# A fused attention, soft mixture of experts and gated output kernel: the last tile's scores moved ahead, seven groups of unread products taken out, another order of the tail, and another pace of weight loads

## The chip, the cores and the metric

The kernel runs on one core of a Trainium2 chip. The metric is the time of one execution on the device, in microseconds (us); of several runs the median counts. A core has five engines that run their own queues of instructions in order and wait for each other by semaphores: TensorE (PE in the profile; PEld is its loading of weights), VectorE (DVE), ScalarE (ACT), GpSimd (POOL) and SyncE (SP), whose queue here holds nothing but the issues of data transfers (DMA).

## What is computed

The reference has three stages: an attention within chunks of 64 positions, a soft mixture of 8 experts with 4 slots each, and a feed-forward layer whose hidden values go through a softmax gate and a normalisation.

```python
# attention: 8 x 8 heads, 576 positions in chunks of 64, head size 64
attn = softmax(q_c @ k_c.T / sqrt(64)); x = attn @ v_c            # -> x: 4608 x 512
# soft mixture of experts, phi: 512 x 32
logits = x @ phi
d = exp(logits - logits.max(0)); d /= d.sum(0) + 1e-09             # over all 4608 tokens
slot_input = d.T @ x                                               # 32 slots x 512
for e in range(8):                                                 # 512 -> 1024 -> 512
    slot_out[e] = relu(slot_input[e] @ w1[e]) @ w2[e]
c = exp(logits - logits.max(1)); c /= c.sum(1) + 1e-09
x = c @ slot_out
# feed-forward with a softmax gate
h = x @ w_in; solu = h * softmax(h)
ln = (solu - mean) / sqrt(var + 1e-06) * g_ln
out = ln @ w_out
```

The softmax over all tokens (`d`) means that no expert can start before every tile of the attention has been seen.

## The kernel before, in words

**The loop (to about 130 us).** The 4608 tokens are 36 tiles of 128 (`NT = 36`). Step i of the loop, for i from 0 to 33, works on several tiles at once: scores S of tile i (`pe_S`, TensorE), row maxima, subtraction and exponential (`mx`, `sub` on VectorE, `exp` on ScalarE), transposed probabilities of tile i-1 (`PT`, evacuated by `PTe`), the product with the values of tile i-2 (`x`, with its row sums `rz`, their reciprocal `rc` and the scaling `xm`), and the transposition and logits of tile i-3 (`xT`, `xTe`, `LT`). Every four tiles a block of logits is closed by a running maximum, an exponential and a product with x that is added up in `acc`. Beside that, GpSimd, ScalarE and VectorE turn the output layer's weights into another format (`sq`, `t`, `u`, `m`, `a`, `add`, `mul`). `STEP` gives the order of these operations for four steps, after which it repeats.

**The loads.** All transfers are issued from SyncE, in the order of the program: q and k of tile i+4 (`qk`, two halves of 256 KB), values for two tiles (`v`, 520 KB), output weights (`raw`, 512 KB), and the experts' weights: 64 tiles `w` of 512 KB. At each step `W` issues `PACE[i+1] - PACE[i]` of these 64. They go into a ring of 23 buffers; the next 19 go into buffers of the loop as these are given up (the operations `own_c`, `own_q`, `own_v`, `own_p`, `own_t`, `own_x`), and the last 22 into ring buffers that the experts have read. A transfer whose buffer is still being read blocks every transfer behind it in SyncE's queue.

**The tail (126 to 148 us), written out by hand.** The steps of the last tiles are single operations with names, registered by `op(name, names of what must stand ahead)`; the string `ORDER` lists them all, and they are emitted in that order. So `ORDER` sets the order of each engine's queue, and nothing else does. The names that matter here:
- S34, S35: scores of the last two tiles. mx34, sub34, exp34; mx35 and, in halves, sub350, sub351, exp350, exp351. PT33, PT34, PT350, PT351 and ptev..: transposed probabilities and their evacuation on ScalarE. x32 to x34, x350, x351: the products with the values. rz.., ev..: row sums (ScalarE), then reciprocal and scaling (VectorE). xT.., xtev.., LT..: transposition, its evacuation, logits.
- lte7, L7, lall7, tm7 close block 7; lte8, L8, lall8, tm8 and lte83, L83, lall83 close block 8; mT8, mn8, Ls, mnl find the maximum, mb spreads it, d7, d8 subtract it, de7, de8 take the exponential, mc and al give the factor for what was summed before. sl70 to sl81 and z8 are the products with d, acc80, acc81 and zacc8 add them up, zt, zr, si0, si1 and siT give the experts' input.
- hz0, hz1 write zeros into two banks of PSUM (ScalarE). px closes a pool and emits nothing.
- id0 to id6: products of the unit matrix with itself, written into places of PSUM that nothing reads before they are written again.
- cq1 to cq7 (GpSimd) sum the output weights, cm0 and cm1 (TensorE) average them, cme (VectorE) copies the average, cms0 to cms7 (GpSimd) subtract it from the 8 blocks of weights, px0 to px7 (VectorE) take each block's largest value, px8 the largest of these, wmt (TensorE) transposes it and wmv (VectorE) makes the scale of it.

**The experts (148 to 187 us).** Two groups of four experts; each `w1_..` or `w2_..` is 8 instructions of 4 x 512, four experts side by side in the array. Between them stand the transpositions of the hidden values, and on VectorE the combine weights (cz0 to cz5) and the maxima px. In `ORDER` this part reads, in the kernel before:

```python
... zr si0 si1 siT open2 cm1 w1_000 w1_001 cme rl00 w1_010
cz0 cms2 cms3 ht00 w1_011 he00 cms6 cz1 cms4 rl01 px2 w2_000 cms7 ht01 px7 w2_001 cms0 cz2 cz3 px6 cz4 cms5 px3 cz5
he01 w2_010 w2_011 so0 px4 px5 cms1 w1_100 px1 w1_101 px0 sot0 late ch0 cl0 px8 wmt ch2 cl2 wmv ct0 ch1 w1_110 rl10
```

**The output layer (to the end).** For each tile: hidden values h, exponential, gate, two 16 bit parts, their transposition by DMA, and 24 products of 128 x 512 (L1396), then the output.

Of the kernel before, what the change touches and what calls it, by code (L numbers as in the profile page):

```python
# [44 lines left out]
ORDER = """
cq1 cq2 cq3 cq4 cq5 cq6 cq7 S34 loadw xT31 PT33 xtev31 x32 own_c mx34 rz32 LT31 sub34 ev32 S35 ptev33 lte7 mx35 exp34
sub350 PT34 x33 ptev34 xT32 L7 exp350 rz33 xtev32 own_q sub351 x34 ev33 PT350 exp351 id0 rz34 ptev0 xT33 PT351 LT32
lall7 tm7 x350 ptev1 x351 xtev33 ev34 xT34 LT33 id1 xtev34 own_v rz35 rc35 LT34 id2 ev350 ev351 xT350 px lte8 xT351
id4 xtev350 xtev351 L8 tm8 LT35 id5 mT8 lte83 mn8 own_p Ls L83 id6 own_t mnl hz1 lall83 mb lall8 cm0 mc id3 d7 d8 de7
hz0 sl71 de8 al sl70 own_x z8 sl80 zacc8 sl81 zt acc80 acc81 zr si0 si1 siT open2 cm1 w1_000 w1_001 cme rl00 w1_010  # L50
cz0 cms2 cms3 ht00 w1_011 he00 cms6 cz1 cms4 rl01 px2 w2_000 cms7 ht01 px7 w2_001 cms0 cz2 cz3 px6 cz4 cms5 px3 cz5
he01 w2_010 w2_011 so0 px4 px5 cms1 w1_100 px1 w1_101 px0 sot0 late ch0 cl0 px8 wmt ch2 cl2 wmv ct0 ch1 w1_110 rl10
cl1 hi0 ct1 ch3 hi1 lo0 ht10 he10 ch4 cl3 ce0 hi6 ce1 ct2 ce2 w1_111 cpt cpe rl11 ch5 wc48 hi3 ct3 ht11 hi4 cl4 ce3
hi5 wc49 hi7 cl5 ct4 lo3 wc50 wc51 ch6 he11 ce4 cl6 wc52 wc53 lo2 ct6 wc54 wc55 ch8 ct5 hi2 ce6 soc0 wc56 soe0 wc57
ch7 soct0 cl7 ct7 ce5 ce7 wc58 cl8 wc59 soce0 wc60 wc61 soc2 soct2 wc62 wc63 soc3 lo1 sw0 soct3 soce2 sw1 soce3 sw2
pev0 pev1 ct8 end2 ce8 f_open f_turn f_h0 f_m0 f_h1 f_m1 f_mm f_e0 f_sc f_g1 f_g0 rp0 f_dg f_e1 f_u0 f_T0 f_u1 s4h0
f_k0 f_T1 f_Te0 f_k1 f_Te1 B0a f_km f_ul0 f_E f_ul1 rp1 s4h1 B0b B0c B0d f_s1 Av1 s4l0 s4l1 Au1 Hm2 B0 Hm3 Al1 Hx2 Hs2
He2 Aq1 B1 f_mean Av2 Au2 f_v1 Hx3 Hm4 He3 Al2 Hs3 Av3 Hx4 Au3 B2 f_v0 S0 Al3 As1 He4 Hm5 Aq2 Av4 C0 Aq3 Hm6 Hs4 Hx5
Hs5 Au4 C1 Al4 As2 He5 Av5 B3 Au5 Hx6 He6 As3 Hm7 Hs6 Aq5 Al5 Aq4 Av6 Au6 B4 C2 As4 Hx7 As5 He7 Hs7 Al6 Av7 Au7 C3 Aq6
Aq7 As6  # L60
"""


# [1437 lines left out]
```

## Time and profile before

| | us |
|---|---|
| median of 3 runs | 404.35 |
| lowest, highest | 404.04, 406.44 |
| the profiled execution, in all | 406.2 |
| its span, first to last instruction | 404.4 |

Busy time in the profiled execution: TensorE 385.9 us (95% of the span), VectorE 311.5 (77%), ScalarE 223.8 (55%), GpSimd 199.4 (49%). The data engines move 407 to 411 GB/s in most slices up to 182 us, and 130 to 166 after it.

Times in the rows count from the span's start. A row of the timeline gives start, duration, engine, line, operation, what is written and read, shapes and the number of instructions merged; the bracket behind it says how long the engine was idle before it and what ended that. Matmuls are pipelined, and their ends are modelled: a row overlaps the next one a little. A float32 matmul of the program is two rows' worth of instructions in the trace.

### The profile page before, as it was taken

To read this page: it belongs to the slowest core of one execution; us is meant where nothing else is said; L and a number is where in the kernel's file an instruction comes from. 1 tells how busy PE (TensorE), PEld (TensorE's weight loads), DVE (VectorE), ACT (ScalarE), POOL (GpSimd) and SP (SyncE) were. 2 spreads that over 40 slices of the span, in tenths; PEclk is the share of its full clock that TensorE was granted. 3 is DMA by queue.
4 is the path that set the end of the run, shared out by engine and by line. 5 is a ranking of instruction groups with operands and counts; after the bars stand their busy time and mean duration, and the time that the engine had idled before them with its cause. 6 is when DMAs were issued, how large, how long until landed. Compare 5 with 4: busy or idle time off the path is not lost. (4 is left out here: it accounts for less than half of the span.)

```text
span 404.4 us, 10343 instructions
## 1 busy us (share of the span) xinstructions
PE 385.9 (95%) x3961; PEld 223.0 (55%) x3961; DVE 311.5 (77%) x777; ACT 223.8 (55%) x470; POOL 199.4 (49%) x201
## 2 busy tenths in 40 slices
PE   3798999999999999999999999999999999999997
PEld 2676777877787752355544444444444444444445
DVE  3588788888987447683989789999888888888840
ACT  1487777877776512231576765556545545455521
POOL 2377677777778428240113235555545445454430
PEclk9999999999999999999999999999999999999999
DMA  7999999999999999993056756778657786567661
GB/s 231 361 411 409 407 407 408 409 397 387 403 361 347 404 398 402 408 410 82 15 98 151 130 134 140 166 166 160 144 132 135 156 130 143 133 143 156 131 157 52
DMA packets 101153, 99.20 MB, mean 245 GB/s; under 512 B 78064, under 2 KB 78704, under 8 KB 101104
## 3 DMA queue, kind: packets, MB, share of 16 engines
q1 hardware_dynamic: 101104, 98.54, 77.9%
q8 instruction: 31, 0.51, 0.5%
q14 instruction: 18, 0.15, 0.1%
HBM read 70.60 MB, written 9.44 MB: 198 GB/s over the span
## 5 line engine op out<-in xcount | busy, mean ns | idle before, releaser
L1197 POOL TENSOR_SCALAR uh<-u,sc 128x1024 f16<-128x1024 f32 (+1 forms) x35 | 65.0, 1857 | 51.2 <-issue 38.3
L1396 PEld LDWEIGHTS <-uhT 128*128 128x128 f16 x560 | 52.2, 98 | 68.6 <-issue 9.0
L1396 PE MATMUL o_ps<-xb,uhT 128*128 128x512 f16 x280 | 66.6, 380 | 0.8 <-DMA uhT<-uh 0.8
L1396 PE MATMUL o_ps<-xb,ulT 128*128 128x512 f16 x280 | 66.3, 379 | 0.0
L1396 PE MATMUL o_ps<-wo,uhT 128*128 128x512 f16 x280 | 66.1, 379 | 0.0
L1325 ACT ACTIVATE e<-h_ps,nm 128x1024 f32<-128x1024 f32 x34 | 37.8, 1112 | 43.9 <-DVE nm L1319 43.9
L1213 ACT ACTIVATE e<-u,nmean 128x1024 f32<-128x1024 f32 x35 | 40.1, 1147 | 28.7 <-DVE nmean L1212 28.7
L257 PE MATMUL s_ps<-qk 128*64 128x128 f32 x576 | 42.4, 291 | 10.8 <-DMA qk<-in_qkT 7.3
L1363 POOL TENSOR_TENSOR a<-a,mhalf 128x1 f32<-128x1 f32 x36 | 21.7, 604 | 56.6 <-DVE a L1380 42.7
L1319 DVE TENSOR_REDUCE nm<-h_ps 128x1 f32<-128x1024 f32 x34 | 41.5, 1220 | 9.7 <-PE h_ps L1314 9.7
L1188 DVE SCALAR_TENSOR_TENSOR u<-h_ps,e 128x1024 f32<-128x1024 f32 x35 | 42.8, 1223 | 6.1 <-ACT e L1325 6.1
L1396 PEld LDWEIGHTS <-ulT 128*128 128x128 f16 x280 | 27.3, 98 | 33.1 <-issue 0.3
L1373 DVE SCALAR_TENSOR_TENSOR ul<-u,sc,uh 128x1024 f16<-128x1024 f32 x35 | 45.3, 1295 | 0.0
L257 PEld LDWEIGHTS s_ps<-qk 128*64 128x64 f32 x576 | 33.1, 144 | 17.9 <-issue 12.1
L266 DVE TENSOR_REDUCE mx<-s_ps 128x8 f32<-128x512 f32 x36 | 24.7, 685 | 12.5 <-PE s_ps L257 12.3
L399 ACT ACTIVATE xt_b<-xt_ps 128x512 f32<-128x512 f32 (+1 forms) x37 | 21.5, 584 | 17.3 <-PE xt_ps L417 16.5
L220 POOL TENSOR_SCALAR conv<-conv 128x256 f32<-128x256 f32 x16 | 17.5, 1096 | 24.6 <-ACT conv L207 24.6
L1414 ACT ACTIVATE ob<-o_ps,a 128x512 f32<-128x512 f32 x35 | 23.7, 678 | 9.5 <-PE o_ps L1396 8.0
L1314 PE MATMUL h_ps<-s,c4T 128*128 128x512 f32 x68 | 27.6, 488 | 0.0
L278 ACT ACTIVATE p<-p 128x512 f32<-128x512 f32 x35 | 21.7, 620 | 6.7 <-DVE p L272 6.7
L272 DVE TENSOR_TENSOR p<-s_ps,mx 128x512 f32<-128x512 f32 x35 | 24.1, 690 | 0.9
L230 POOL TENSOR_TENSOR conv<-conv 128x256 int32<-128x256 int32 x32 | 23.3, 727 | 2.6
(234 smaller groups left out, 637.8 us busy)
## 6 DMA issues: line engine op xcount, KB each, us to landing
w<-in_w SPq DMA_DIRECT2D x45, 512.0 KB, 8.3
qk<-in_qkT SPq DMA_DIRECT2D x72, 256.0 KB, 7.0
vall<-in_v SPq DMA_DIRECT2D x18, 520.0 KB, 7.6
out<-ob SPq DMA_DIRECT2D x35, 256.0 KB, 2.1
raw<-in_w SPq DMA_DIRECT2D x16, 512.0 KB, 7.6
qk<-in_w SPq DMA_DIRECT2D x4, 512.0 KB, 9.6
w_raw<-in_w SPq DMA_DIRECT2D x3, 512.0 KB, 9.3
vall<-in_w SPq DMA_DIRECT2D x3, 512.0 KB, 9.0
```

The lines of the kernel that those rows point to most:

```text
L257: nc.tensor.matmul(s[ts(c, 64), ts(g, 128)], b[:, 1, ts(2 * g + c, 64)], b[:, 0:3:2, ts(2 * g + c, 64)], start=True, stop=True, tile_posit ...
L266: mark("mx", nc.vector.tensor_reduce(out=mx, in_=s, axis=AX.X, op=ALU.max))
L272: mark("sub", nc.vector.tensor_tensor(out=p, in0=s, in1=mx.unsqueeze(2).to_broadcast([128, 8, 64]), op=ALU.subtract,))
L1188: nc.vector.scalar_tensor_tensor(out=u, in0=d["h"], scalar=1.0, in1=e, op0=ALU.mult, op1=ALU.mult, accum_out=zz[:, 1:2])
L1197: nc.gpsimd.tensor_scalar(out=uh[:, 0:n], in0=u[:, 0:n], scalar1=d["sc"][:, 1:2], scalar2=1.0, op0=ALU.mult, op1=ALU.mult)
L1213: nc.scalar.activation(out=d["e"], in_=d["u"], func=AF.Square, bias=nmean, scale=1.0, accum_out=d["zz"][:, 2:3])
L1314: nc.tensor.matmul(h[:, ts(n, 512)], c4T[:, i, :], s4[n], start=True, stop=True)
L1319: nc.vector.tensor_reduce(out=nm, in_=st[i]["h"], axis=AX.X, op=ALU.max, negate=True)
L1325: nc.scalar.activation(out=d["e"], in_=d["h"], func=AF.Exp, bias=d["nm"], scale=1.0, accum_out=d["zz"][:, 0:1])
L1373: nc.vector.scalar_tensor_tensor(out=ul, in0=d["u"], scalar=d["sc"][:, 1:2], in1=d["uh"], op0=ALU.mult, op1=ALU.subtract)
L1396: nc.tensor.matmul(d["o"], lt(n % 8), w(n % 8), start=(n == 0), stop=(n == 23))
L1414: nc.scalar.activation(out=ob, in_=d["o"], func=AF.Copy, scale=d["a"][:, 7:8])
```

## The change

Four edits, all in tables and in the tail; no operation of the computation is added or removed.

1. `ORDER`: S35 stands directly behind S34, and the list from there to the experts' first products is another one. Among what moved: mx35 ahead of sub34; x33 ahead of PT34; rz34 and ev34 ahead of tm7, which now stands behind ev351; xT34 ahead of x351; d7 ahead of mc; al and de8 ahead of hz0; z8 between sl80 and sl81; cm1 behind w1_000 and w1_001, where it stood ahead of both. From cme on the list is the same.
2. The operations id0 to id6 and the function `idle` are gone: 12 products of 128 x 128 on TensorE.
3. `PACE` is raised by one or two tiles at most of its entries from 18 to 33. Entry 34 and the ring of 23 are the same.

```diff
 PACE = [
-    0, 0, 1, 1, 2, 3, 3, 4, 4, 5, 6, 6, 7, 7, 8, 9, 9, 10, 10, 11, 12, 12, 13, 13, 14, 15, 15, 16,
-    16, 17, 18, 18, 19, 22, 25, 25,
+    0, 0, 1, 1, 2, 3, 3, 4, 4, 5, 6, 6, 7, 7, 8, 9, 9, 10, 11, 11, 12, 13, 14, 14, 15, 16, 16, 17,
+    18, 19, 19, 20, 21, 23, 25, 25,
 ]
...
-cq1 cq2 cq3 cq4 cq5 cq6 cq7 S34 loadw xT31 PT33 xtev31 x32 own_c mx34 rz32 LT31 sub34 ev32 S35 ptev33 lte7 mx35 exp34
...
+cq1 cq2 cq3 cq4 cq5 cq6 cq7 S34 S35 loadw xT31 mx34 mx35 PT33 x32 xtev31 rz32 ptev33 sub34 LT31 lte7 ev32 own_c exp34
...
-    def idle(o, n):
-        for _ in range(n):
-            nc.tensor.matmul(o, ident, ident, start=True, stop=True)
-
-    op("id0", "PT350")(lambda: idle(T["pt"][:, 2, :], 2))
-    op("id1", "LT33 id0")(lambda: idle(lt_t[last][:, 3, :], 2))
-    op("id2", "LT34 id1")(lambda: idle(lt_t[last][:, 3, :], 2))
-    op("id4", "xT351 ev34 id2")(lambda: idle(sx[:, 0, 256:384], 1))
-    op("id5", "LT35 id4")(lambda: idle(sx[:, 0, 256:384], 1))
-    op("id6", "L83 lte8 id5")(lambda: idle(lt_t[last][:, 0, :], 2))
-    op("id3", "cm0 mnl ev34 id2")(lambda: idle(sx[:, 0, 256:384], 2))
```

Line numbers of the changed kernel are one smaller up to here and twelve smaller behind the removed lines.

**VectorE in the tail.** The names: mx are the maxima (mx34, mx35), `p<-s_ps,mx` is sub34, `xl` are the halves of tile 35, RECIPROCAL and the row behind it are ev32, ev33 and ev34, `tm<-L_ps` is tm7. In the kernel before:

```order
L266 TENSOR_REDUCE mx<-s_ps 128x8
L272 TENSOR_TENSOR p<-s_ps,mx 128x512
L604 RECIPROCAL rz<-rz 128x8
L607 TENSOR_TENSOR xb_84<-x_ps,rz 128x2x4x64
L266 TENSOR_REDUCE mx<-s_ps 128x8
L545 TENSOR_TENSOR xl_152<-s_ps,mx 128x256
L545 TENSOR_TENSOR xl_153<-s_ps,mx 128x256
L604 RECIPROCAL rz<-rz 128x8
L607 TENSOR_TENSOR xb_85<-x_ps,rz 128x2x4x64
L366 TENSOR_REDUCE tm<-L_ps 128x32
L604 RECIPROCAL rz<-rz 128x8
L607 TENSOR_TENSOR xb_86<-s_ps,rz 128x2x4x64
```

In the changed kernel:

```order
L265 TENSOR_REDUCE mx<-s_ps 128x8 x2
L271 TENSOR_TENSOR p<-s_ps,mx 128x512
L603 RECIPROCAL rz<-rz 128x8
L606 TENSOR_TENSOR xb_84<-x_ps,rz 128x2x4x64
L544 TENSOR_TENSOR xl_153<-s_ps,mx 128x256
L544 TENSOR_TENSOR xl_152<-s_ps,mx 128x256
L603 RECIPROCAL rz<-rz 128x8
L606 TENSOR_TENSOR xb_85<-x_ps,rz 128x2x4x64
L603 RECIPROCAL rz<-rz 128x8
L606 TENSOR_TENSOR xb_86<-s_ps,rz 128x2x4x64
```

Both maxima now stand together, and tm7 no longer stands between ev33 and ev34 (xb_85 and xb_86).

**TensorE at the start of the experts.** `s_ps<-cs,acc` is si0 and si1, `cm_ps` is cm1, `h_ps<-w,xl` are the first products with experts' weights (16 of them are w1_000 and w1_001). In the kernel before:

```order
L846 MATMUL zt_ps<-cs,zacc 128x32
L857 MATMUL s_ps<-cs,acc 128x32 x4
L827 MATMUL cm_ps<-csum,mean_l 128x256
L939 MATMUL h_ps_2581<-w,xl_152 4x512 x16
L939 MATMUL h_ps_2582<-w,xl_152 4x512 x8
L964 MATMUL hT_ps<-cs,xb_85 128x128 x4
```

In the changed kernel:

```order
L834 MATMUL zt_ps<-cs,zacc 128x32
L845 MATMUL s_ps<-cs,acc 128x32 x4
L927 MATMUL h_ps_2567<-w,xl_152 4x512 x16
L815 MATMUL cm_ps<-csum,mean_l 128x256
L927 MATMUL h_ps_2568<-w,xl_152 4x512 x8
L952 MATMUL hT_ps<-cs,xb_85 128x128 x4
```

cm1 moved behind the first 16 products with weights.

**SyncE at the end of the loop.** qk are loads of q and k (the last row of them, qk3, is tile 35), vall of values, w of experts' weights. In the kernel before:

```order
L177 DMA qk0_111<-in_qkT 64x1024 x2
L129 DMA w_1993<-in_w12 128x1024
L182 DMA vall_123<-in_v1 128x1040
L177 DMA qk1_112<-in_qkT 64x1024 x2
L129 DMA w_2051<-in_w12 128x1024
L177 DMA qk2_113<-in_qkT 64x1024 x2
L182 DMA vall_123<-in_v1 128x1040
L177 DMA qk3_114<-in_qkT 64x1024 x2
L129 DMA w_2209<-in_w12 128x1024
```

In the changed kernel:

```order
L176 DMA qk3_114<-in_qkT 64x1024 x2
L128 DMA w_1940<-in_w12 128x1024
L176 DMA qk0_111<-in_qkT 64x1024 x2
L128 DMA w_1997<-in_w12 128x1024
L181 DMA vall_123<-in_v1 128x1040
L176 DMA qk1_112<-in_qkT 64x1024 x2
L176 DMA qk2_113<-in_qkT 64x1024 x2
L128 DMA w_2117<-in_w12 128x1024
L181 DMA vall_123<-in_v1 128x1040
L176 DMA qk3_114<-in_qkT 64x1024 x2
L128 DMA w_2213<-in_w12 128x1024
```

One more w stands ahead of qk0 (tile 32), one behind qk2 (tile 34) where none stood, and of the five that followed qk3 (tile 35) three are left.

## Rows read from the trace of the kernel before

**Rows 1.** The chain that ended last (start us, us, what), its long run of products

```profile
210.10 5.35 PE o_ps L1396 x24
```

**Rows 2.** Busy time by stretches: PE, PEld, DVE, ACT, POOL; PEclk, DMA share, GB/s

```profile
0.00:20.00 20.00, 11.18 (x140) 9.11 (x141) 9.12 (x19) 6.03 (x13) 5.67 (x14) 1.00 0.85 295
...
115.00:120.00 5.00, 4.97 (x105) 4.17 (x105) 4.26 (x10) 3.80 (x12) 3.70 (x5) 1.00 0.92 332
120.00:125.00 5.00, 4.77 (x103) 3.32 (x100) 4.83 (x15) 3.58 (x11) 3.98 (x5) 1.00 0.86 303
...
155.00:160.00 5.00, 5.00 (x48) 1.38 (x44) 4.96 (x6) 2.28 (x3) 5.00 (x4) 1.00 1.03 406
160.00:165.00 5.00, 5.00 (x52) 1.23 (x48) 4.93 (x10) 1.08 (x3) 0.05 (x1) 1.00 1.02 405
```

**Rows 3.** Timeline of TensorE in the tail: S34, and the unread product id2

```profile
126.02 1.09 PE L257 MATMUL s_ps<-qk 128*64 128x128 f32 x16
...
138.17 0.71 PE L646 MATMUL lt_ps<-cs 128*128 128x128 f32 x4
```

**Rows 4.** Timeline of ScalarE in the tail: rz34, lall7, lte8, hz0, al

```profile
133.77 0.19 ACT L305 ACTIVATE rz<-s_ps 128x8 f32<-128x8 f32 x1
...
134.61 0.27 ACT L361 ACTIVATE lall<-L_ps 128x128 f32<-128x128 f32 x1
...
138.98 0.49 ACT L346 ACTIVATE ltb<-lt_ps 128x384 f32<-128x384 f32 x1 [1.39 <-PE lt_ps L646]
...
143.48 0.58 ACT L817 ACTIVATE h_ps<-cs 128x512 f32<-128x512 f32 x1
...
144.20 0.28 ACT L457 ACTIVATE al<-mc 128x1 f32<-128x1 f32 x1
```

**Rows 5.** Timeline of VectorE in the tail: tm7, then the reciprocal of ev34

```profile
134.92 0.29 DVE L366 TENSOR_REDUCE tm<-L_ps 128x32 f32<-128x128 f32 x1 [0.78 <-ACT lall L361]
135.12 0.19 DVE L604 RECIPROCAL rz<-rz 128x8 f32<-128x8 f32 x1
```

**Rows 6.** Timeline from cm1 to wmt: TensorE, VectorE and GpSimd

```profile
147.49 0.68 PE L827 MATMUL cm_ps<-csum,mean_l 128*128 128x256 f32 x2
148.10 5.33 PE L939 MATMUL h_ps<-w,xl 128*4 128x512 f32 x48
...
147.69 0.29 DVE L863 TENSOR_TENSOR xl<-s_ps,zr 128x128 f32<-128x128 f32 x1 [0.25 <-PE s_ps L857]
148.21 0.69 DVE L400 COPY acc<-cm_ps 128x512 f32<-128x512 f32 x1 [0.22 <-PE cm_ps L827]
...
148.98 11.07 POOL L834 TENSOR_TENSOR wo<-wo,acc 128x512 f32<-128x512 f32 x8 [13.19 <-DVE acc L400]
...
156.35 1.27 DVE L1059 TENSOR_REDUCE wmx<-wo 128x1 f32<-128x512 f32 x2
...
165.26 0.15 DVE L1066 TENSOR_REDUCE wmx<-wmx 128x1 f32<-128x8 f32 x1
...
167.17 0.14 PEld L1071 LDWEIGHTS wm_ps<-cs,wmx 128*128 128x128 f32 x1
```

**Rows 7.** Loads of tile 29 and of the last weights, and who reads them

```profile
L177 SPq DMA_DIRECT2D qk<-in_qkT x2: 477/480/484, 98.1 to 98.8; - x2
DMA to landing us min/median/max: 7.6/7.6/7.6
...
107.76 1.09 PE L257 MATMUL s_ps<-qk 128*64 128x128 f32 x16
...
L129 SPq DMA_DIRECT2D w<-in_w x1: 327/327/327, 174.9 to 174.9; - x1
DMA to landing us min/median/max: 10.2/10.2/10.2
...
185.76 1.08 PE L990 MATMUL h_ps<-w,hTb 128*4 128x128 f32 x32
```

**Rows 8.** Timeline of TensorE at the program's start: the first scores

```profile
5.20 1.97 PE L257 MATMUL s_ps<-qk 128*64 128x128 f32 x16 [5.20 <-DMA qk<-in_qkT]
```

More of the change, by code (lines that the diff above doesn't have):

```diff
@@ L45 @@
 ORDER = """
-cq1 cq2 cq3 cq4 cq5 cq6 cq7 S34 loadw xT31 PT33 xtev31 x32 own_c mx34 rz32 LT31 sub34 ev32 S35 ptev33 lte7 mx35 exp34
[L47 to L60, printed above, removed]
+cq1 cq2 cq3 cq4 cq5 cq6 cq7 S34 S35 loadw xT31 mx34 mx35 PT33 x32 xtev31 rz32 ptev33 sub34 LT31 lte7 ev32 own_c exp34
@@ new lines @@
+x33 own_q PT34 ptev34 xT32 L7 rz33 sub351 sub350 x34 exp350 PT350 exp351 ev33 xtev32 ptev0 xT33 PT351 lall7 LT32 rz34
+x350 ptev1 ev34 xtev33 xT34 x351 xtev34 rz35 LT33 rc35 LT34 ev350 ev351 tm7 lte8 px xT350 xT351 own_v L8 tm8 xtev350
+xtev351 LT35 lte83 mT8 mn8 own_p Ls own_t L83 mnl lall8 lall83 hz1 mb d7 mc de7 al cm0 d8 de8 sl70 hz0 sl71 sl80 z8
+acc80 sl81 own_x zacc8 acc81 zt si0 si1 zr siT open2 w1_000 w1_001 cm1 cme rl00 w1_010 cz0 cms2 cms3 ht00 w1_011 he00
+cms6 cz1 cms4 rl01 px2 w2_000 cms7 ht01 px7 w2_001 cms0 cz2 cz3 px6 cz4 cms5 px3 cz5 he01 w2_010 w2_011 so0 px4 px5
@@ new lines @@
+cms1 w1_100 px1 w1_101 px0 sot0 late ch0 cl0 px8 wmt ch2 cl2 wmv ct0 ch1 w1_110 rl10 cl1 hi0 ct1 ch3 hi1 lo0 ht10 he10
+ch4 cl3 ce0 hi6 ce1 ct2 ce2 w1_111 cpt cpe rl11 ch5 wc48 hi3 ct3 ht11 hi4 cl4 ce3 hi5 wc49 hi7 cl5 ct4 lo3 wc50 wc51
+ch6 he11 ce4 cl6 wc52 wc53 lo2 ct6 wc54 wc55 ch8 ct5 hi2 ce6 soc0 wc56 soe0 wc57 ch7 soct0 cl7 ct7 ce5 ce7 wc58 cl8
+wc59 soce0 wc60 wc61 soc2 soct2 wc62 wc63 soc3 lo1 sw0 soct3 soce2 sw1 soce3 sw2 pev0 pev1 ct8 end2 ce8 f_open f_turn
+f_h0 f_m0 f_h1 f_m1 f_mm f_e0 f_sc f_g1 f_g0 rp0 f_dg f_e1 f_u0 f_T0 f_u1 s4h0 f_k0 f_T1 f_Te0 f_k1 f_Te1 B0a f_km
@@ L61 @@
+f_ul0 f_E f_ul1 rp1 s4h1 B0b B0c B0d f_s1 Av1 s4l0 s4l1 Au1 Hm2 B0 Hm3 Al1 Hx2 Hs2 He2 Aq1 B1 f_mean Av2 Au2 f_v1 Hx3
+Hm4 He3 Al2 Hs3 Av3 Hx4 Au3 B2 f_v0 S0 Al3 As1 He4 Hm5 Aq2 Av4 C0 Aq3 Hm6 Hs4 Hx5 Hs5 Au4 C1 Al4 As2 He5 Av5 B3 Au5
+Hx6 He6 As3 Hm7 Hs6 Aq5 Al5 Aq4 Av6 Au6 B4 C2 As4 Hx7 As5 He7 Hs7 Al6 Av7 Au7 C3 Aq6 Aq7 As6
 """
```

## Prediction, written before the changed kernel was run

> **What bounds the kernel now.** I read the views from the end backwards. The chain of work that ended last runs, from 210.10 us to the last instruction, through TensorE's products L1396 alone, 24 of them in 5.35 us for the first tile of that run [rows 1]. The change touches none of that code, so whatever it does has happened by 210 us, and a shift of the expert stage (148 to 187 us) arrives at the end unchanged.
>
> Next the busy time by stretches. From 155 to 165 us TensorE is busy 5.00 of each 5 us, and VectorE 4.96 and 4.93 [rows 2]. So in the expert stage two engines are full at once, and TensorE paces it. The loads are nearly as long: they move about 406 GB/s, but 332 and 303 in the stretches 115 to 120 and 120 to 125 us [rows 2]. The last weight tile is issued at 174.9 us and lands 10.2 us later, at 185.1 [rows 7]; the products that read it begin at 185.76 [rows 7]. So weights are 0.7 us ahead of TensorE at their closest: they do not hold it up, but little is to spare.
>
> Last the timeline of the tail of the loop (126 to 148 us) and of the first 20 us of the experts, instruction by instruction [rows 3 to 6].
>
> **The sum, part by part.** It goes against the profiled execution's span of 404.4 us. That execution took 406.2 us in all, the median of the runs is 404.35 us; I carry the difference found over to the median.
>
> *Scores of tile 35 ahead.* S35 takes the place 1.03 us after S34 in which tile 31 was transposed (S34 starts at 126.02 us [rows 3]; its 1.09 us overlap the next start by a little). So xT31, PT33, x32, LT31 and what hangs on them start about 1.03 later. In return S35's old place, behind LT31, closes. Does the delay reach the end of the tail? The next thing that everything waits for is ev34, on VectorE. In the kernel before its reciprocal came at 135.12, although the sums it reads (rz34 on ScalarE) were done at 133.77 + 0.19 = 133.96 [rows 4, 5]: ahead of it in VectorE's queue stood tm7, which waited for lall7 until 134.92 [rows 5]. The new list puts tm7 behind ev351. Now rz34 stands behind lall7 on ScalarE (134.61 before, so about 134.9 [rows 4]), and the reciprocal follows at about 135.1. The 1.16 us of slack take up the 1.03: net 0. Bounds: 0 to +0.5 (the part by which x34, in the same chain, may be late).
>
> *Unread products out.* Most of the 12 stand in gaps of TensorE. One pair does not: id2 writes the tile lt_ps at 138.17 us, and lte8 on ScalarE waits for it until 138.98, 1.39 us idle [rows 3, 4]. Without it lte8 can start at about 138.3; since the transposes of tile 35 still stand ahead of L8 on TensorE, I count 0.4 of the 0.7. Behind that is the chain L8, tm8, mT8, mn8, mnl, mb. Bounds: 0.2 to 0.7.
>
> *Order of d7, mc, al, hz0.* In the kernel before ScalarE writes a zero bank (hz0, 143.48, 0.58 us) ahead of de8 and al (144.20), and z8 needs both [rows 4]. The new list has al and de8 ahead of hz0, and d7 ahead of mc. Up to 0.4 us; TensorE's sl7 products fill most of that time, so I count 0.15 (0 to 0.4). The tail together: -0.55 us, between -1.1 and +0.3. siT ends, and the first weights' products start, at about 147.55 instead of 148.10.
>
> *cm1 behind w1_001.* This is the part that costs. cm1 ran at 147.49, in TensorE's wait for siT (147.69 to 147.98), and the 48 first rows of weights began at 148.10 [rows 6]: it cost nothing. Its reader cme started on VectorE at 148.21, and on it hangs GpSimd, which stood idle 13.19 us for it and then subtracted the mean from 8 blocks in 11.07 us, 1.38 each [rows 6]. Now 32 of the 48 rows are ahead of cm1, 5.33 x 32/48 = 3.55 us. cm1 takes 0.68, so cme starts 4.2 to 4.25 us behind the first weights' product instead of 0.11: about 4.1 late. GpSimd has nothing else to do and cannot catch up. The fifth block it finishes is block 7, at 148.98 + 5 x 1.38 = 155.9 in the kernel before. Its reader px7 is the second of the pair that starts at 156.35 (1.27 us for two [rows 6]), so at 156.98: 1.08 us of slack. With 4.1 more, VectorE waits at px7 for 4.1 - 1.1 = 3.0 us, counted from the start of the weights. Behind px7 in VectorE's queue stand cz3, px6, cz4, px3, cz5, four more maxima and px8 (165.26, 0.15 us), with no idle time between them (4.93 of 5 us busy [rows 2, 6]). So px8 ends at 165.41 + 3.0 = 168.4. TensorE loads px8's result as a weight at 167.17 [rows 6]; it had 1.65 us to spare there after the 0.1 a semaphore takes. Now it comes to that place 0.45 us later (cm1's own place in its stream, half of 0.68 being overlapped) and finds nothing until 168.5 to 168.6: +1.4 us against the kernel before, counted from the start of the weights. Everything behind it in the stage is TensorE's own pace. Lower bound 0.45 us, if VectorE has room that I don't see; upper 2.0, if the two engines slow each other now that they work at once more.
>
> *Pace of the loads.* From step 18 on, one or two more weight tiles are issued early, and the five that came at once behind the last scores are three. Two more tiles now stand ahead of the last load of values, and so keep the transfers going while that load waits for its buffer. The missing rate, (406 - 332) x 5 + (406 - 303) x 5 = 885 KB, is 2.2 us of loading: the last weight may land up to 2.2 us sooner. Since TensorE did not wait for it, that pays nothing. It covers the 0.55 us by which TensorE comes sooner, which the 0.7 us of room would have covered too. The price is on the loads behind: 512 KB at 400 GB/s are 1.28 us. The tightest is tile 29: its second half is issued at 98.8 and lands 7.6 later, at 106.4, and its scores start at 107.76 [rows 7], 1.4 us of slack; 0.1 is left. 0 us, at most +1.3 if both early tiles fall ahead of it.
>
> *TensorE's clock.* The granted clock is 1.00 in every stretch read, the first 20 us included [rows 2], but durations do not agree with that: the 16 first score rows take 1.97 us at 5.20, after 5.20 us of idleness, and 1.09 us at 126.02 [rows 3, 8]. So the lower of the two levels (1.2 against 2.4 GHz) is seen in durations alone, and the engine had stood idle before it. In the tail without the unread products I find, by the same working, no gap over about 0.5 us. I count 0. The Trainium skill, "TensorE: Matmul & The Clock Gate", section "Why this matters for your kernels", speaks against the removal: it advises to keep the engine busy and to leave no idle gaps between bursts of matmuls, since an idle engine goes back to half rate. By that rule the sum would be that of the third rival below; the trace agrees that idleness goes with the slow level, and no row of it shows a fall in midstream.
>
> Sum: 0 - 0.4 - 0.15 + 1.4 + 0 + 0 = +0.85 us, so 404.35 + 0.85 = 405.2 us; the profile's span about 405.25.
>
> **The rivals.** *VectorE makes up for cme.* If the chain from px7 to px8 has room, only cm1's 0.45 stays: -0.55 + 0.45 = -0.1, 404.25 us. For it: px8 was done 1.65 us ahead of its reader. Against it: the queue is full from 155 to 165 us, and the delay is 3.0.
>
> *Loads held the experts after all.* Then the 2.2 us come through: 402.2 us, and cme's delay is beside the point. For it: 0.7 us of room is thin. Against it: TensorE is busy 5.00 of 5 us in the stage.
>
> *The clock falls (the slower side).* Place: the products from sl7 to si1, some 3.7 us of TensorE's time on the path, and perhaps the 48 weights' rows (5.33 us). At 1.97/1.09 = 1.8 times, +2.9 to +7 on top of the forecast: 408.2 to 412 us. It decides if TensorE falls back before the weights begin. For it: the 12 products hold up no result, so what they do is keep the engine busy. Against it: the gaps they leave are short.
>
> *Early weights push the scores' loads.* Tile 29 waits 1.3 us, and the loop with it: 405.2 + 1.3 = 406.5 us. For it: 0.1 us of slack. Against it: every other tile from 18 on has more.
>
> **How the numbers follow.** Forecast 0.63; VectorE makes up 0.14; loads held it 0.08; clock 0.07; late scores 0.08. The likeliest case gives 405.2 us, with its own range 404.6 to 406. The range 403.5 to 407 holds it, the first rival and the late scores (0.85 together) and takes in the bounds (-1.1 + 0.45 = -0.65 below, 0.3 + 2.0 above); the other two stay out. A difference within 1% (4 us) is about what a measurement of this kernel cannot tell from none: faster by more 0.02 (loads with a better tail), slower by more 0.07 (the clock), the rest, 0.91, within.
>
> **What would show it.** Right: siT about 0.55 us sooner; lte8 no longer waiting for a product of TensorE; cme 4 us behind the first weights' row; VectorE idle about 2.5 us ahead of the second px row, released by GpSimd; TensorE waiting about 1 us for px8 ahead of the transpose wm_ps; no dip in the rate at 115 to 125 us, and the last weight landing 2 us sooner. Wrong: no idle time of VectorE at px7, matmuls of about 1.8 times their length in the tail, or a wait of the scores for qk near 108 us.

## The result, and the profile after

The changed kernel takes 408.57 us (median of 6 runs, 407.43 to 410.07), beside 405.43 us of the kernel before (6 runs, 404.04 to 406.44): a ratio of 1.008, with a 95% interval of 1.0059 to 1.0101. It lost 3.1 us where 0.85 was forecast, and lies above the range. Of the 3.4 us between it and the forecast of 405.2 us, 1.1 are the base: the forecast was added to 404.35 us, the median of three runs, where six give 405.43; a range moved up by this would still end below it, at 408.1. How often TensorE's clock falls differs between the changed kernel's executions, as their mean granted clock shows: not at all (1.0) in the two shortest, 407.43 and 408.34 us, once (0.996) in three, twice (0.992) in the profiled one (410.07 us, span 408.3), which is the longest.

I cut both profiles at the same five marks: the start of S34, of the first weights' products, of the transposition wm_ps, of the first product o_ps, and the end of TensorE's last instruction. All in us:

| kernel | to S34 | S34 to weights | weights to wm_ps | wm_ps to o_ps | o_ps to end |
|---|---|---|---|---|---|
| before | 126.02 | 22.08 | 19.18 | 29.13 | 205.16 |
| after | 124.10 | 21.40 | 23.24 | 30.84 | 205.82 |

The first column is no part of the change: the scores of tile 5, up to which both programs are alike, start at 23.60 us before and at 22.09 after, and in the experiments S34 starts anywhere between 123.8 and 126.0 us (in two profiles of one and the same kernel, b_no_unread, at 125.98 and 124.88). The rest adds up to -0.68 + 4.06 + 1.71 + 0.66 = +5.75 us, and less the 1.92 of the first column to the 3.8 by which TensorE's end is later.

TensorE after, in timeline rows (start, duration, then as before); they answer to [rows 1, 3, 6]:

```profile
124.10 1.97 PE L256 MATMUL s_ps<-qk 128*64 128x128 f32 x32
...
145.50 5.31 PE L927 MATMUL h_ps<-w,xl 128*4 128x512 f32 x32 [0.48 <-DVE xl L851]
150.74 0.70 PE L815 MATMUL cm_ps<-csum,mean_l 128*128 128x256 f32 x2
...
168.74 0.32 PE L1059 MATMUL wm_ps<-cs,wmx 128*128 128x128 f32 x1 [1.47 <-DVE wmx L1054]
...
208.28 1.90 PE L1384 MATMUL o_ps<-xb,uhT 128*128 128x512 f16 x8 [1.56 <-DMA uhT<-uh]
```

The 32 rows ahead of cm1 take 5.31 us, where 48 rows took 5.33 [rows 6]. The windows tell why; columns as in [rows 2]:

```profile
115.00:120.00 5.00, 5.00 (x108) 4.12 (x106) 4.31 (x10) 3.99 (x12) 4.11 (x5) 1.00 0.99 386
120.00:125.00 5.00, 4.76 (x82) 3.44 (x84) 4.54 (x13) 3.27 (x10) 4.18 (x6) 1.00 1.02 407
144.00:146.00 2.00, 1.52 (x18) 1.12 (x21) 1.08 (x4) 0.00 (x0) 0.00 (x0) 0.99 1.03 391
146.00:148.00 2.00, 2.00 (x16) 0.43 (x12) 0.00 (x0) 0.00 (x0) 0.00 (x0) 0.50 1.04 405
168.00:170.00 2.00, 0.87 (x5) 0.55 (x5) 1.60 (x7) 0.00 (x0) 0.00 (x0) 0.96 1.04 414
170.00:172.00 2.00, 2.00 (x14) 0.41 (x16) 0.72 (x2) 0.60 (x1) 0.00 (x0) 0.50 1.02 406
```

The granted clock is 0.50, the lower level (1.2 of 2.4 GHz), in 146 to 148 and again in 170 to 172 us. Ahead of each fall TensorE had been idle: for siT (1.52 busy of 2 us), and for px8 (0.87 of 2). The first two rows answer to [rows 2]: the dip of the loads' rate is gone, 386 and 407 GB/s for 332 and 303.

VectorE, ScalarE and GpSimd after; they answer to [rows 4 to 6]:

```profile
136.37 0.49 ACT L345 ACTIVATE ltb<-lt_ps 128x384 f32<-128x384 f32 x1 [0.48 <-PE lt_ps L311]
...
151.48 0.69 DVE L399 COPY acc<-cm_ps 128x512 f32<-128x512 f32 x1 [6.13 <-PE cm_ps L815]
...
152.25 11.07 POOL L822 TENSOR_TENSOR wo<-wo,acc 128x512 f32<-128x512 f32 x8 [18.38 <-DVE acc L399]
...
159.64 0.69 DVE L1047 TENSOR_REDUCE wmx<-wo 128x1 f32<-128x512 f32 x1 [3.06 <-POOL wo L822]
...
162.10 1.27 DVE L883 TENSOR_SCALAR cz<-cz 128x36 f32<-128x36 f32 x1
...
168.53 0.15 DVE L1054 TENSOR_REDUCE wmx<-wmx 128x1 f32<-128x8 f32 x1
```

cme starts 5.98 us behind the first weights' row (0.11 before), px7 waits 3.06 us for GpSimd, and px8 is done 23.2 us behind the weights' start, where TensorE finds nothing for 1.47 us.

Last, the DMA queues while the first two tiles of the output layer are transposed (packets, MB, share; then us to landing). After, 200.5 to 209 us:

```profile
q8 instruction: 1, 0.02, 0.6%
issues: line engine op xcount, KB each, median us to landing
uhT<-uh SPq DMA_TRANSPOSE x1, 4.7
```

Before, 198 to 206 us, where the queue of instructions has no row:

```profile
q1 hardware_dynamic: 2112, 0.52, 35.4%
uhT<-uh SPq DMA_TRANSPOSE x1, 3.1
```

In the changed kernel a piece of code is fetched just then, and the transposition lands 1.6 us later. Over the whole profile of the changed kernel, the 27 transpositions uhT beside which no such fetch runs land in 3.05 to 3.21 us, and the 8 beside which one runs in 3.05 to 4.68. The kernel before has a wait of this kind too, one tile later and shorter, and the changed kernel has none there; so the stretch grows by 0.66 us and not by 1.56:

```profile
210.10 1.90 PE L1396 MATMUL o_ps<-xb,uhT 128*128 128x512 f16 x8 [0.78 <-DMA uhT<-uh]
```

### The profile page after: what moved, and what is told of

The parts are those of the page before. It is cut to its first block, busy times and chain, and to the rows that moved or that the text cites. A ratio compares the mean times of both kernels' runs of the same rounds, so it can differ in the third digit from the quotient of the medians.

```text
span 408.3 us, 10299 instructions
## 1 busy us (share of the span) xinstructions
PE 386.7 (95%) x3937; PEld 220.7 (54%) x3937; DVE 311.1 (76%) x777; ACT 224.1 (55%) x470; POOL 199.8 (49%) x201
## 4 chain that ended last, share of the span: by engine, by line
PE 72%; DMA 10%; issue 7%; ACT 5%; DVE 4%; POOL 2%; POOLq 0%; ACTq 0%; DVEq 0%
PE o_ps L1384 43%; PE s_ps L256 7%; DMA qk<-in_qkT 6%; PE h_ps L1302 4%; PE h_ps L927 3%; PE xt_ps L416 3%; PE x_ps L282 2%; DMA w<-in_w 2%; PE sl_ps L467 2%; PE lt_ps L325 2%; PE pt_ps L407 2%; DVE p L271 2%; DVE mx L265 2%; POOL xb L1070 1%; PE o_ps L1394 1%
## 5 line engine op out<-in xcount | busy, mean ns | idle before, releaser
L282 PE MATMUL x_ps<-vall,pt 64*64 64x65 f32 x1088 | 24.1, 227 | 0.4 <-ACT ltb L341 0.4
```

Of the source, the lines that this page charges most:

```text
L282: nc.tensor.matmul(x[ts(c, 64), a, ts(g, 65)], pt[ts(a, 64), ts(c, 64)], vall[ts(a, 64), i % 6, ts(2 * g + c, 65)], start=True, stop=True, ...
```

## The experiments

The stretches of each from S34 on, from the profiled execution, with the time and the ratio to the kernel before on the same chip (95% interval):

| kernel | S34 to weights | to wm_ps | to o_ps | to end | us | ratio |
|---|---|---|---|---|---|---|
| a_cm1_ahead | 21.39 | 19.17 | 29.14 | 205.71 | 405.15 | 0.9995 (0.9981 to 1.0009) |
| a_unread | 22.68 | 21.53 | 30.82 | 204.94 | 409.12 | 1.0096 (1.0073 to 1.0120) |
| a_cm1_unread | 23.21 | 19.17 | 29.13 | 205.02 | 406.02 | 1.0024 (1.0010 to 1.0038) |
| b_no_unread | 21.00 | 19.17 | 29.13 | 205.76 | 406.66 | 1.0038 (1.0020 to 1.0057) |
| b_no_unread_again | 21.06 | 19.17 | 30.16 | 205.90 | 405.30 | 1.0003 (0.9978 to 1.0029) |
| b_cm1_behind | 22.11 | 21.53 | 30.83 | 205.01 | 408.72 | 1.0096 (1.0064 to 1.0129) |
| b_pace | 22.29 | 19.17 | 29.14 | 205.01 | 406.19 | 1.0018 (0.9981 to 1.0054) |
| b_short | 21.89 | 19.18 | 29.13 | 205.05 | 404.15 (profiled) | 0.9992 (0.9959 to 1.0025) |
| a_cm1_short | 24.40 | 19.17 | 29.14 | 204.87 | 406.55 (profiled) | 1.0060 (1.0015 to 1.0104) |
| a_cm1_early | 21.58 | 19.18 | 33.16 | 205.66 | 406.61 | 1.0035 (1.0007 to 1.0062) |
| a_cm1_mid | 20.90 | 19.92 | 29.13 | 205.60 | 405.77 | 1.0022 (1.0001 to 1.0043) |
| a_cm1_ahead_s35 | 20.60 | 19.17 | 29.14 | 205.66 | 404.24 | 0.9972 (0.9948 to 0.9995) |

For the two kernels with short products the time of the profiled execution stands: three of b_short's six executions took 412.97 to 416.53 us and two of a_cm1_short's 412.31 and 412.72, with mean clocks of 0.975 to 0.983. The ratio of b_short is that of its other three executions; that of a_cm1_short leaves out the one of 412.72 us alone.

### cm1 back ahead of the weights

```diff
-siT open2 w1_000 w1_001 cm1 cme
+siT open2 cm1 w1_000 w1_001 cme
```

> The changed kernel with one edit undone: cm1 stands ahead of w1_000 again, in TensorE's wait for siT. Theory 1 (place of cm1: it lets VectorE wait for GpSimd at px7 and TensorE for px8 at the transpose wm_ps, and the clock falls only as a consequence): no idle time of VectorE at px7, none of TensorE at wm_ps, no half clock at 170 us; the time falls by about 3.5 us, from 408.6 to 405.0. Theory 2 (the unread products' absence lets the clock fall, wherever cm1 stands): 32 rows of weights still take 5.3 us instead of 3.55 at the start of the experts; cm1's own +1.4 us goes, 1.8 us stays: 406.5 to 407. Theory 3 (something in the loop or in the output layer): 408 or more.

405.15 us: 3.4 us of the loss are gone with this one edit, as theory 1 has it; theories 2 and 3 fall for the bulk. TensorE:

```profile
145.05 0.68 PE L815 MATMUL cm_ps<-csum,mean_l 128*128 128x256 f32 x2
145.69 5.33 PE L927 MATMUL h_ps<-w,xl 128*4 128x512 f32 x48
164.86 0.27 PE L1059 MATMUL wm_ps<-cs,wmx 128*128 128x128 f32 x1
```

48 rows take 5.33 us again, and nothing waits at wm_ps. The clock stays up without the unread products: the mean is 0.999 or 1.0 in all twelve executions.

### The unread products back, cm1 left behind

```diff
-exp351 ev33 ... LT33 rc35 LT34 ev350 ... xT351 own_v ... LT35 lte83 ... L83 mnl ... cm0 d8
+exp351 id0 ev33 ... LT33 id1 rc35 LT34 id2 ev350 ... xT351 id4 own_v ... LT35 id5 lte83 ... L83 id6 mnl ... cm0 id3 d8
```

> The changed kernel with the 12 unread products put back at the places in the list that answer to their old ones (id0 behind exp351, id1 behind LT33, id2 behind LT34, id4 behind xT351, id5 behind LT35, id6 behind L83, id3 behind cm0); cm1 stays behind w1_001. Theory 2 (the clock): the 32 first rows of weights take 3.55 us again, no fall to the lower level at 146 us, cme 4.1 us behind the first weights' row instead of 6.0, TensorE waits about 1 us at wm_ps: 408.6 - 1.8 (48 rows at the lower level) - 1 (the later cme) = 405.8 to 406.3. Theory 1: the clock still falls at 145.5, since TensorE still idles 0.5 us for siT: 408.5 or a little more. Theory 3: 408.5.

409.12 us: the products save nothing. Yet the fall at the first weights is not in this profile, so it separates the two sizes:

```profile
148.07 3.62 PE L938 MATMUL h_ps<-w,xl 128*4 128x512 f32 x32 [0.47 <-DVE xl L862]
151.62 0.70 PE L826 MATMUL cm_ps<-csum,mean_l 128*128 128x256 f32 x2
...
169.60 0.32 PE L1070 MATMUL wm_ps<-cs,wmx 128*128 128x128 f32 x1 [1.45 <-DVE wmx L1065]
```

With 32 rows at full clock, weights to wm_ps takes 21.53 us, 2.35 more than before, and the wait at wm_ps is the same 1.45 us. Behind it the clock falls here too:

```profile
168.00:170.00 2.00, 0.47 (x3) 0.13 (x1) 1.88 (x7) 0.60 (x1) 0.00 (x0) 1.00 1.03 410
170.00:172.00 2.00, 1.69 (x8) 0.81 (x12) 1.10 (x5) 0.56 (x1) 0.00 (x0) 0.59 1.03 410
```

That fall costs 30.82 - 29.13 = 1.69 us in the next stretch. The expectation had counted 2.8 us for the fall at the first weights; it is worth 23.24 - 21.53 = 1.71, and the second one stands beside it, with or without the unread products. Neither comes in every execution: in three of these six the mean clock is 1.0, and they are the shortest (407.61 to 408.38 us).

### Both undone

> The changed kernel with both undone: cm1 ahead of w1_000 and the 12 unread products back. What is left of the change is S35's place, the other list and the pace. If cm1 and the clock hold all of the loss (theories 1 and 2 alike), the tail's gain is left: 405.4 - 0.3 to - 0.7 = 404.7 to 405.1. If theory 3 (loop, loads or output layer) has a share, more than 405.5.

406.02 us, more than forecast, and above the 405.5 past which the expectation gave theory 3 a share. The stretches put it elsewhere, in the tail: in the new list the unread products lengthen the tail (23.21 us against 21.39), so the tail's gain rested on taking them out.

### The kernel before without the unread products

> The kernel before without the 12 unread products, nothing else. Theory 2: the gaps they leave let the clock fall in the tail or at the first weights, as in the changed kernel: +1.8 us for 48 rows at the lower level, less up to 0.4 us (lte8 no longer waits for id2): 406.8 to 407.2. Theory 1: TensorE has cm1 in its wait for siT, the clock holds, and lte8 gains up to 0.4 us: 405.0 to 405.4.

Its mean clock is 1.0 in all twelve executions, so theory 2 is out as a cause. The profile shows a tail of 21.00 us, 1.08 shorter, and a loss behind the first o_ps row, where TensorE waits as in the changed kernel:

```profile
203.94 1.25 PE L1384 MATMUL o_ps<-xb,uhT 128*128 128x512 f16 x5 [1.50 <-DMA uhT<-uh]
```

Its queues, 197 to 206 us, show the fetch:

```profile
q8 instruction: 1, 0.02, 0.7%
uhT<-uh SPq DMA_TRANSPOSE x2, 3.9
```

The 3.9 is the median of two; the one beside the fetch lands after 4.64 us. That is a gain of 0.5 us on balance, and the time of 406.66 us does not agree. A second series of the same kernel followed.

> The kernel before without the 12 unread products a second time, since its time (406.66) and its profile do not agree: by the profile's stretches it gains 1.08 us in the tail and loses 0.6 behind the first o_ps row, so 405.0. If the loss of 1.2 us is the kernel's own: again 406.4 to 406.9, and a stretch of the profile shows it. If it came from the loads of the loop in those executions, which this kernel shares with the kernel before: 404.9 to 405.5.

405.30 us, equal to the kernel before. The loss of 1.2 us did not come back. The second profile repeats the tail (21.06 us) and the end (205.90 us); its 30.16 us from wm_ps to o_ps, 1.03 more than elsewhere, hold a stop of TensorE of 0.50 us (see "cm1 early"). Where the first series lost its time stays open: its profiled execution was among its shortest, and shows the 0.5 us gained. The two intervals share 1.0020 to 1.0029, so a small loss is not ruled out.

### The kernel before with cm1 behind

```diff
-siT open2 cm1 w1_000 w1_001 cme
+siT open2 w1_000 w1_001 cm1 cme
```

> The kernel before with one edit of the change alone: cm1 behind w1_000 and w1_001. Theory 1, as the traces so far size it: from the first weights' row to the transpose wm_ps 21.5 us without a fall of the clock at the first weights (23.2 with one) instead of 19.17, VectorE idle 3 us for GpSimd at px7, then in some runs the half clock for 1.7 us more behind the wait at wm_ps: 405.4 + 2.4 to + 4.1 = 407.8 to 409.5. The prediction's size for it was + 1.4: 406.8. If the loss of cm1's place needs the change's list or its loads: 405.5 to 406.5.

408.72 us, ratio 1.0096: this edit alone gives a loss as large as that of the whole change, with the old list, the old pace and the unread products in place. VectorE:

```profile
150.32 0.69 DVE L400 COPY acc<-cm_ps 128x512 f32<-128x512 f32 x1 [4.34 <-PE cm_ps L827]
...
158.46 0.69 DVE L1059 TENSOR_REDUCE wmx<-wo 128x1 f32<-128x512 f32 x1 [3.06 <-POOL wo L834]
...
160.92 1.27 DVE L895 TENSOR_SCALAR cz<-cz 128x36 f32<-128x36 f32 x1
...
167.35 0.15 DVE L1066 TENSOR_REDUCE wmx<-wmx 128x1 f32<-128x8 f32 x1
```

Again 21.53 us to wm_ps, and then the fall (granted clock 0.50 from 170 to 172 us), 1.70 us.

### The pace alone

```diff
-    0, 0, 1, 1, 2, 3, 3, 4, 4, 5, 6, 6, 7, 7, 8, 9, 9, 10, 10, 11, 12, 12, 13, 13, 14, 15, 15, 16,
+    0, 0, 1, 1, 2, 3, 3, 4, 4, 5, 6, 6, 7, 7, 8, 9, 9, 10, 11, 11, 12, 13, 14, 14, 15, 16, 16, 17,
...
```

> The kernel before with the pace of the loads of the changed kernel, nothing else. Predicted 0 for this term: 405.4, with the dip of the rate at 115 to 125 us gone and TensorE unchanged. Rival: the early weights hold up scores' loads (up to + 1.3: 406.7), or the weights held the experts after all (- 2.2: 403.2).

No difference that the measurement can tell (0.9981 to 1.0054). That rules out the gain of 2.2 us (0.9946), but by itself not the loss of 1.3 us (1.0032) of the late scores. The profile speaks against that one: from 90 us on TensorE waits for no load of q and k, and S34 starts at 125.07 us, sooner than before. The rate is 410 and 404 GB/s in 115 to 120 and 120 to 125 us, and every stretch of TensorE is within 0.21 us of the one before: more transfers early paid nothing, as predicted.

### Unread products of 16 columns

```diff
-            nc.tensor.matmul(o, ident, ident, start=True, stop=True)
+            nc.tensor.matmul(o[:, 0:16], ident, ident[:, 0:16], start=True, stop=True)
```

> The kernel before with the 12 unread products 16 columns wide instead of 128: as many instructions in TensorE's queue, at the same places, hardly any time. Theory 4 (taking 24 instructions out of the queue shifts the point at which the next piece of code is fetched by a DMA, so that this falls onto the transposing DMA of uh at 199 us, and the second tile's products wait 1.5 us): no such fetch between 197 and 206 us, 205.1 us from the first o_ps row to the end as in the kernel before (205.7 without the products), tail 0.7 to 1.0 us shorter: 404.4 to 404.8. If the unread products are of use for the clock: 406 or more, as without them (406.66).

> The changed kernel with cm1 ahead of w1_000 again and the 12 unread products back, 16 columns wide. Theory 4: 205.1 us from the first o_ps row to the end instead of 205.7, the tail 21.4 to 21.7 us: 0.4 to 0.7 less than the same without the products (405.15), 404.5, faster than the kernel before by 0.9. If the fetch is not moved by the number of instructions: 405.2 to 405.4.

Theory 4 holds in its point on the fetch: with as many instructions as before, o_ps to the end takes 205.05 and 204.87 us. By all profiles it goes by that number: the seven profiles with the products show 204.87 to 205.16 us, the seven without 205.60 to 205.90. In all fourteen the fetch starts behind nearly the same number of TensorE's recorded instructions, 6070 to 6086, which with the products falls within 0.4 us of the first o_ps row, and without them (47 or 48 records fewer) 5.9 to 6.4 us behind it. The times were missed: these short products take almost as long as the wide ones (four instructions of id1 hold the queue for 0.55 us instead of 0.64, and the tail of b_short is 21.89 us), and in a_cm1_short's profiled execution the clock falls in the tail itself:

```profile
140.00:142.00 2.00, 2.00 (x14) 1.61 (x15) 0.90 (x5) 1.11 (x4) 0.00 (x0) 1.00 1.03 397
142.00:144.00 2.00, 2.00 (x18) 1.33 (x22) 0.60 (x4) 1.18 (x4) 0.00 (x0) 0.71 1.02 397
144.00:146.00 2.00, 2.00 (x19) 0.87 (x11) 0.26 (x1) 0.00 (x0) 0.00 (x0) 0.50 1.05 400
```

The engine had run the short products among its others until then, and its rows leave no gap (2.00 of 2 us).

### cm1 early

```diff
-... al cm0 d8 ... siT open2 w1_000 w1_001 cm1 cme
+... al cm0 cm1 d8 ... siT open2 w1_000 w1_001 cme
```

> The changed kernel with cm1 directly behind cm0, ahead of the products sl: the average is there early, but TensorE stands idle in the wait for siT, as in the changed kernel. Theory 1a (the clock falls at the first weights because TensorE idles ahead of them, 0.48 us for siT behind shorter waits): cme is early, VectorE does not wait at px7 and TensorE not at wm_ps, but the 32 first rows of weights still take 5.3 us in part of the executions: 405.15 + 0.5 (cm1 ahead of the sl products) + up to 1.7 = 405.7 to 407.4. Theory 1b (the fall belongs to cm1's late place): 32 rows in 3.6 us, 405.2 to 405.7.

In the profile the 48 rows take 5.33 us although TensorE idled 0.48 us ahead of them, so this wait does not always make the clock fall. The time of 406.61 us lies in the range of theory 1a, but does not prove it: five of the twelve executions have a mean clock below 0.999 (406.94 to 410.03 us), the other seven have a median of 405.59, and only of the profiled one is it known where the clock fell. What that one lost is another thing:

```profile
182.00:184.00 2.00, 0.24 (x8) 0.00 (x0) 0.05 (x1) 0.00 (x0) 0.00 (x0) 1.00 0.01 1
184.00:186.00 2.00, 1.48 (x26) 0.95 (x29) 0.78 (x2) 0.00 (x0) 0.00 (x0) 0.94 0.04 8
186.00:188.00 2.00, 2.00 (x36) 1.42 (x32) 0.78 (x2) 0.11 (x1) 0.00 (x0) 0.50 0.00 0
```

```profile
164.93 0.27 PE L1059 MATMUL wm_ps<-cs,wmx 128*128 128x128 f32 x1
...
184.14 1.04 PE L978 MATMUL h_ps<-w,xb 128*4 128x128 f32 x21 [1.90 <-issue]
```

In the middle of a run of products TensorE stood for 1.90 us without waiting for anything the profile shows, and then the clock fell: 4.0 us in all. In b_no_unread_again the same place shows 0.50 us. Such stops have a pattern. The fourteen profiles hold 18 of more than 0.2 us, at five places of TensorE's queue alone: behind 706, 3010, 3521, 4801 and 5825 of its recorded instructions, which lie multiples of 256 apart (to within one). Each ends 1.2 to 1.5 us behind the end of a fetch of code, one packet of 16 KB. So TensorE most likely stood waiting for its own next piece of code; the fetch ahead of the 1.90 us took 2.6 us, where it takes 1.0 to 1.3 at that place in the other profiles.

### cm1 half way

```diff
-siT open2 w1_000 w1_001 cm1 cme
+siT open2 w1_000 cm1 w1_001 cme
```

> The changed kernel with cm1 between w1_000 and w1_001, half way. By the prediction's working: cme 0.11 + 1.78 + 0.6 us behind the first weights' row, 2.4 later than in the kernel before, of which px7 has 1.08 of slack; VectorE waits 1.3 us, cz4 0.7 us longer, px8 2.0 to 2.4 later, against 1.65 + 0.6 us that TensorE has to spare at wm_ps: from the first weights' row to wm_ps 19.8 to 20.0 us, and 406 us without a fall of the clock at the first weights, 407.7 with one. If the price went with the place in proportion: half of 3.4, 406.9.

19.92 us to wm_ps, inside the 19.8 to 20.0 of the expectation; in proportion it would have been 20.4 (19.18 and half of 2.35). VectorE:

```profile
147.96 0.69 DVE L399 COPY acc<-cm_ps 128x512 f32<-128x512 f32 x1 [2.71 <-PE cm_ps L815]
...
156.11 0.69 DVE L1047 TENSOR_REDUCE wmx<-wo 128x1 f32<-128x512 f32 x1 [0.58 <-POOL wo L822]
...
158.56 1.27 DVE L883 TENSOR_SCALAR cz<-cz 128x36 f32<-128x36 f32 x1
...
165.01 0.15 DVE L1054 TENSOR_REDUCE wmx<-wmx 128x1 f32<-128x8 f32 x1
```

VectorE waits 0.58 us at px7, where 1.3 was expected, and px8 comes 2.46 us later than in the kernel before. It still ends ahead of TensorE's need at 165.31 us: nothing waits at wm_ps, and the clock holds at 168 to 172 us. The 0.75 us above 19.17 are therefore cm1's own place in TensorE's queue (0.45 in the prediction); cme's delay, here 2.46 us, costs nothing as long as it stays within the room at wm_ps.

### S35 in its old place, cm1 ahead

```diff
-S34 S35 loadw xT31 mx34 mx35 PT33 ... LT31 lte7 ev32 own_c
+S34 loadw xT31 mx34 PT33 ... LT31 S35 lte7 ev32 mx35 own_c
```

> The changed kernel with cm1 ahead of w1_000 again, and S35 behind LT31 with mx35 behind ev32, as in the kernel before. The prediction counted S35's place at 0 to + 0.5 us. If the place costs nothing: 405.15, and 21.4 us from S34 to the first weights' row. If it is what makes the new list's tail longer than the old one's without the unread products (21.39 against 21.00): 404.8 and 21.0 us.

404.24 us, ratio 0.9972 (0.9948 to 0.9995): the shortest of all, 0.05 to 0.5% ahead of the kernel before. Its tail is 20.60 us, and x33 starts 4.71 us behind S34. With S35 ahead, x33 has to wait and starts 5.04 us behind it, in a_cm1_ahead:

```profile
129.34 0.70 PE L282 MATMUL x_ps<-vall,pt 64*64 64x65 f32 x32 [0.41 <-ACT ltb L341]
...
135.41 0.46 PE L282 MATMUL x_ps<-vall,ptl 64*64 64x65 f32 x14 [0.26 <-issue]
```

The second row is a stop of TensorE inside x351, behind 4801 of its recorded instructions, one of the five places above; the changed kernel's profile has it as well and a_cm1_mid's has not. By these single profiles the place of S35 costs 20.90 - 20.60 = 0.30 us (a_cm1_mid), and the tail is 0.79 us longer in an execution with the stop.

## Why the prediction was wrong, point by point

**The mechanism was right, its price was not.** The step that failed is "cm1 behind w1_001", counted at +1.4 us with 2.0 as its upper bound; it measured 2.35. cme came 4.18 us late without the clock's fall (a_unread), as worked out. Three terms behind it were off. The rows of the first two, in the kernel before and then in the changed kernel (cz1 is `lall<-lall,cz`, cz4 is `cz<-cz`, `wo<-wo,acc` are GpSimd's blocks):

```profile
148.98 6.23 POOL L834 TENSOR_TENSOR wo<-wo,acc 128x512 f32<-128x512 f32 x5 [13.19 <-DVE acc L400]
154.67 1.76 DVE L890 TENSOR_TENSOR lall<-lall,cz 128x1152 f32<-128x1152 f32 x1
155.15 2.42 POOL L834 TENSOR_TENSOR wo<-wo,acc 128x512 f32<-128x512 f32 x1
159.52 0.57 DVE L895 TENSOR_SCALAR cz<-cz 128x36 f32<-128x36 f32 x1
```

```profile
152.25 7.36 POOL L822 TENSOR_TENSOR wo<-wo,acc 128x512 f32<-128x512 f32 x5 [18.38 <-DVE acc L399]
154.50 1.48 DVE L878 TENSOR_TENSOR lall<-lall,cz 128x1152 f32<-128x1152 f32 x1
154.73 2.40 POOL L822 TENSOR_TENSOR wo<-wo,acc 128x512 f32<-128x512 f32 x1
```

First, px7's wait. GpSimd's blocks do not take 1.38 us each: seven take 1.26 to 1.30, and the one that meets cz1 on VectorE takes 2.4. In the kernel before that is the sixth, so block 7, the fifth, is done 6.23 us behind GpSimd's start, at 155.21 and not at 155.9, and px7 (156.94) had 1.73 us of slack, not 1.08. With cm1 behind, GpSimd starts later and cz1 does not, so the long block is the third, and block 7 takes 7.34 us (a_unread). The wait is then 4.18 - 1.73 + 1.11 = 3.56 us instead of 3.0.

Second, cz4, which stands behind px7: it takes 1.26 us instead of 0.57. In all fourteen profiles its row ends 0.04 to 0.05 us behind the end of GpSimd's last block, whether it takes 0.28 us (a_cm1_early), 0.57 or 1.27, so it stands until that block is done. The Trainium skill, "SBUF — State Buffer", section "SBUF: two separate sides", says that the two engines share one pair of ports under an exclusive lock, and that a VectorE instruction with two inputs in SBUF, or in a mode that uses two ports, and a GpSimd instruction that reads there exclude each other: the later one waits for the whole instruction of the other. The rows of cz1, which has two inputs, fit that both ways: in all fourteen profiles cz1 ends 1.21 to 1.22 us behind the GpSimd block that it meets, and the long block 1.14 to 1.16 us behind cz1. Whether cz4, with one input, runs in such a mode is not shown.

Third, what TensorE had to spare was 1.81, not 1.65: px8 stood 17.16 us behind the weights' start [rows 6], wm_ps follows 0.21 us behind px8 where it waits for it (169.60 against 169.39), and it started at 19.18. So 3.56 + 0.69 makes px8 4.25 us later (measured: 4.16), and 4.16 - 1.81 is 2.35 us. The prediction had named the two engines slowing each other as the ground of its upper bound, and given it 0.6 us; it is 1.11 + 0.69.

**The clock was counted at nothing.** The prediction held it against the unread products, and looked for the fall between sl7 and the weights; its own sum made TensorE wait "about 1 us" at wm_ps, but no step asked what that idleness does to the clock. In all three profiles with cm1 behind, the clock falls right there, and this costs 1.7 us (30.82 to 30.84 against 29.13). A fall at the first weights, seen in the changed kernel's profile alone, costs 23.24 - 21.53 = 1.71 us more, since it delays cm1, on which everything hangs. The falls are not certain: by the mean clock 6 of the 18 executions of these three kernels had none, 10 had one, 2 had two. The third rival priced the fall at 2.9 to 7 us, where one was worth 1.7 and the two of the profile 3.4, and its cause was wrong: with cm1 ahead and the products gone, the clock stays at 1.00 at both places (a_cm1_ahead, b_no_unread). What makes a fall come in one execution and not in another is open; a wait of 0.48 us for siT stands ahead of the first weights in a_cm1_early and a_cm1_mid too, without a fall there in their profiles. The rule that the prediction cited from the Trainium skill ("TensorE: Matmul & The Clock Gate", section "Why this matters for your kernels"), not to leave idle gaps between bursts of matmuls, fits the falls behind wm_ps (0.47 and 0.87 busy of 2 us), though the waits there are shorter than the gaps that the section warns of; as a warning against taking the products out it is not borne out.

**The tail: right in sum, by luck.** -0.55 was forecast, -0.68 measured, by other terms. The unread products were worth 1.08, not 0.4 (22.08 to 21.00 in the kernel before). S35's place cost 0.30, inside its bounds, and the stop in x351 another 0.49, which nothing had foreseen. What is left for the order of d7, mc, al and hz0 and the rest of the list is 20.60 - 21.00 = -0.40, for -0.15. The working for ev34 held: its reciprocal comes 8.83 us behind S34 (9.10 before), and no longer behind tm7.

**The fetch** is not in the prediction at all: taking instructions out of TensorE's queue moves the moment at which code is fetched, and in this kernel onto the transposition for the second tile: +0.66 us on balance. It eats up the tail's gain, so that a_cm1_ahead ends level with the kernel before.

**The pace** was right: 0, within what the measurement can tell. So was the first rival's ground to be rejected: VectorE did not make up for cme.

Together: -0.68 + 2.35 + 0.66 + 1.7 for each fall, so 2.3 us without one, 4.0 with one and 5.7 with two. The measured loss of the medians, 3.1 us, lies between the first two. The two executions without a fall lost 2.0 and 2.9 us against the median before, so already without the clock the loss is more than twice the forecast; those with one lost 3.1 to 3.5 and that with two 4.6, some 0.5 to 1.1 us less than the sum, and executions of one kernel scatter by 2 us and more (404.04 to 406.44 before). The experiments fit these sizes, except for the first series of b_no_unread.

## What to carry to other kernels

An instruction that sits in another engine's wait costs nothing there, and its new place is priced by following its reader to the end: through each queue, instruction by instruction and not by the mean of a merged row, and with the waits that two engines put on each other once they meet at other places. Where a sum ends in a new wait of TensorE in the middle of its work, add the price of a fall of its clock behind the wait as a chance: here 1.7 us on top of a wait of 1.45, in most executions but not in all. And where a change alters the number of instructions, look in the queue of instruction fetches at what the fetch falls on.
